# Causal masks of two attention chunks, first tile of each unit: from a GpSimd select to a VectorE minimum, with a new set of order offsets

## The chip, the cores and the metric

The kernel runs on one core of one Trainium2 chip. The metric is the device time of one execution in microseconds. The median of five runs before the change is 925.9 us (924.85 to 927.38).

A core has five engines with an instruction queue each, worked in order: TensorE (PE in the profile; its weight loads are shown as PEld), VectorE (DVE), ScalarE (ACT), GpSimd (POOL) and SyncE (SP, which here only issues transfers). They wait for each other through semaphores.

## What is computed

Two layers, each an attention mixer and an MLP with residuals, on 2048 tokens of width 576, in bfloat16. The attention has 32 heads of width 18, is causal, and each query sees its own key and the 255 before it. Cut to what matters:

```python
def _A_ref(x, wqkv, wo):                    # H = 32, Dh = 18, W = 256
    qkv = (x @ wqkv).reshape(B, S, 3, H, Dh).transpose(2, 0, 3, 1, 4)
    q, k, v = qkv[0], qkv[1], qkv[2]
    scores = einsum("bhqd,bhkd->bhqk", q, k) * Dh ** -0.5
    mask = (idx[:, None] - idx[None, :] >= 0) & (idx[:, None] - idx[None, :] < W)
    p = softmax(where(mask, scores, -1e9))
    return einsum("bhqk,bhkd->bhqd", p, v) ... @ wo
def _B_ref(x, w1, b1, w2, b2):              # F = 4608
    return gelu(layernorm(x) @ w1 + b1) @ w2 + b2
x = x + _A_ref(layernorm(x), ...)
x = x + _B_ref(layernorm(x), ...)           # and both once more
```

## The kernel before

**Tiling.** The tokens are cut into 16 tiles of 128, and the tiles into four chunks of four. With two layers there are eight chunks of work, k = 0 to 7; 0 to 3 are the first layer. Weights of the attention stay in SBUF, those of the MLP are streamed by SyncE.

**Attention of one chunk** (function `E`). The heads are taken in eight groups of four. For each group the query and key tiles that meet are packed into three units of up to 512 columns. Scores are computed transposed, with keys on the partitions and queries along the columns. A unit runs through four engines:

- TensorE computes scores (L757) of four heads into two pairs of PSUM banks. Three pairs exist, and the last can also be taken by other work.
- ScalarE takes the exponential of each pair (L766) into one of three buffers of `pT`, in bf16: 128 keys x 4 heads x up to 512 queries. No maximum is subtracted.
- GpSimd zeroes what the mask excludes (L787): a select by an affine function of partition and column. A 128x128 block needs this where queries and keys are of the same tile ("d", the diagonal) or two tiles apart ("o", the edge of the window). Blocks of one kind that lie side by side go in one select: 128x512 elements for one block (four heads), 128x1024 for two. So a unit has one or two selects; in the code `mi` counts them.
- TensorE multiplies the result with the values (L804, 20 columns: 18 of a head and ones that sum the row). These are the P.V matmuls. At the end of a group VectorE takes the reciprocal (L814) and scales (L819) into `attq`.

The P.V matmuls of a unit are placed two units behind its scores. The scores of the unit three later need its `pT` buffer free again.

**Chunks 0 and 1.** In chunk 0 tiles before the sequence's start are missing, so its three units are 384, 512 and 256 columns wide and have five selects in a group: d and o; d over two blocks, and o; d. Chunk 1 has six: d and o over two blocks; d over two blocks and o; o and d. 368 selects run in all.

**Other work.** `qkv` (L671) makes queries, keys and values; VectorE copies them from PSUM (L710 for queries and keys, L697 for values) and SyncE transposes queries and keys by transfer (L729). `tail` transposes `attq` into `attT` (L848), multiplies with the output weights (L671 again, `wo_sb`), adds the residual on VectorE (L838), takes statistics (L592, L594), 1/sigma on GpSimd (L603, L605), normalises on VectorE (L615, and L620 for a last piece of 64 columns that is wanted twice), and transposes into `xnTm` (L635). The MLP is `G_part` (L881 and L893 on TensorE, the gelu on ScalarE L896) and `mm2` (L922, residual L838, or L841 for the last). Warm-up matmuls (L579) fill gaps that the planner expects on TensorE in the first 140 us.

**What sets the order.** No order is written out by hand. Every piece of work is a task with an engine, a cost and a priority; `Plan.schedule` simulates the engines with these costs and writes down each engine's queue. A priority is a formula plus an offset for the task's stage from the table `PL.nudge`; the stages are named after the chunk (`ea1`, `q2.0`, `t0`, ...). A table of other offsets gives other queues on every engine, with the same tasks. Waits follow from the reads and writes named by each task; an engine's instruction waits until all it names are done, and what stands behind it in its queue waits too.

Of the kernel before, what the change touches and what calls it, by code (L numbers as in the profile page):

```python
# [6 lines left out]
BF16 = mybir.dt.bfloat16  # L7
ACT = mybir.ActivationFunctionType
ALU = mybir.AluOpType
P = 128  # L10
# [398 lines left out]
def build_kernel(nc, A_x, A_wqkv, A_wo, B_x, B_w1, B_b1, B_w2, B_b2, out):  # L409
# [32 lines left out]
    PL = Plan(S, 7)  # L442
    add = PL.add


    PL.nudge = {"b": 1.83, "ea0": -1.98, "ld0+": 40.46, "eb0": 2.23, "q1.0": -6.02, "q1.1": 1.09, "t0": 6.35, "ga0": -26.49, "q2.0": 12.46,
                "q2.2": 12.06, "q2.3": 21.72, "t1": -35.56, "ea2": -3.78, "ga1": -4.7, "ma1": 15.69, "ma1+": -9.39, "q3.2": -1.65, "q3.3": -7.2,
                "eb3": 1.74, "ma2": 3.52, "q4.0": 39.31, "q4.2": 6.69, "q4.3": -1.19, "t3": 50.91, "mb2": 75.66, "mb2+": -12.34, "eb4": 2.23,
                "ma3": 19.38, "q5.3": 4.22, "t4": -3.2, "ln6": 1.17, "ga4": 2.93, "ma4": 3.37, "q6.0": 2.8, "q6.1": 2.68, "q6.3": 11.39, "t5": 14.34,
                "gb4": 5.24, "ln7": 19.99, "ea6": 18.52, "mb4": 22.88, "ma5": 16.32, "q7.0": 16.24, "q7.1": 29.31, "q7.2": 33.42, "q7.3": 24.98,  # L450
                "t6": 73.06, "gb5": 28.24, "mb5": 74.41, "ga6": -3.51, "eb7": -2.5, "t7": -1.07}

    def sb(name, shape, dtype):
        return nc.alloc_sbuf_tensor(name, shape, dtype)
# [21 lines left out]
    vtmp = sb("vtmp", [P, NT], FP32)  # L476
    rstd = sb("rstd", [P, NT], FP32)
    warm = sb("warm", [P, 256], BF16)
    ident = sb("ident", [P, P], BF16)
    b1in = sb("b1in", [NF, P], BF16)  # L480
    nhalf = sb("nhalf", [P, 4], FP32)
# [73 lines left out]
    def x_load(a, cnt, reads, prio):  # L555
# [8 lines left out]
    add("dve", lambda e: e.memset(ident[:, :], 1.0), writes=["ident"], cost=0.15, prio=-11)  # L564
    add("pool", lambda e: e.affine_select(ident[:, :], ident[:, :], pattern=[[-1, P]], compare_op=ALU.is_equal, fill=0.0, base=0,
                                          channel_multiplier=1), writes=["ident"], cost=0.3, prio=-10)
    add("pool", lambda e: e.memset(xn[:, :, D:KD * 128], 0.0), writes=[f"xn{i}" for i in range(NXN)], cost=0.4, prio=-10)
    for i in range(NQN):
        add("pool", lambda e, i=i: e.memset(qn[:, i, :].rearrange("p (h e) -> p h e", e=32)[:, :, DH:32], 0.0),
# [175 lines left out]
    def scores(k, g, parts, prio):  # L745
        l, t0, nt = CH[k]
        T0 = l * NT + t0
        qs, qname = q_of(k)
        sl = pcount[0] % PS
        pcount[0] += 1  # L750
        bs = [Bank(SC, True), Bank(SC, True)]

        def fn(e):
            ins = None
            for (so, qo, nq, col) in parts:
                for j in range(4):
                    ins = e.matmul(two(bs[j // 2])[:, j % 2, col:col + nq * 128], k_of(T0 + so)[0][32 * j:32 * j + 32, g, :],  # L757
                                   qs[32 * j:32 * j + 32, g, qo * 128:(qo + nq) * 128], start=True, stop=True, tile_position=(32 * j, 0))
            return ins
        rd = [f"{qname}{qo + i}" for (so, qo, nq, col) in parts for i in range(nq)] + [k_of(T0 + p[0])[1] for p in parts]  # L760
        ncol = sum(p[2] for p in parts) * 128
        add("pe", fn, reads=rd, writes=bs, cost=0.14 + ncol * 0.00053, prio=prio, lat=0.15, alloc=bs, fifo="pa", after=[f"p{sl}h{h}" for h in range(2)] + [f"p{sl}m{m}" for m in range(3)])
        lo = min(p[3] for p in parts)
        hi = max(p[3] + p[2] * 128 for p in parts)
        for h2 in range(2):
            add("act", lambda e, h2=h2: e.activation(pT[:, sl, 2 * h2:2 * h2 + 2, lo:hi], two(bs[h2])[:, :, lo:hi],  # L766
                                                     ACT.Exp, scale=SCALE),
                reads=[bs[h2]], writes=[f"p{sl}h{h2}"], cost=0.07 + 2 * (hi - lo) * 0.00083, lat=0.17,
                fifo="act", prio=prio)
        blk = {}  # L770
        for (so, qo, nq, col) in parts:
            for q in range(nq):
                if qo + q == so:
                    blk[col + q * 128] = "d"
                elif qo + q == so + 2:
                    blk[col + q * 128] = "o"
        runs = []
        for c in sorted(blk):
            if runs and runs[-1][0] == blk[c] and runs[-1][1] + runs[-1][2] * 128 == c:
                runs[-1][2] += 1  # L780
            else:
                runs.append([blk[c], c, 1])
        for mi, (kind, col, nb) in enumerate(runs):
            sgn = 1 if kind == "d" else -1
            pat = [[0, 4]] + ([[0, nb]] if nb > 1 else []) + [[sgn, 128]]
            ap = pT[:, sl, :, col:col + nb * 128]
            add("pool", lambda e, ap=ap, pat=pat, sgn=sgn, kind=kind: e.affine_select(  # L787
                ap, ap, pattern=pat, compare_op=(ALU.is_ge if kind == "d" else ALU.is_gt), fill=0.0, base=0, channel_multiplier=-sgn),
                reads=[f"p{sl}h0", f"p{sl}h1"], writes=[f"p{sl}m{mi}"], cost=0.12 + 0.475 * nb, prio=prio)
        return sl  # L790
# [307 lines left out]
```

The softmax here doesn't subtract the row's maximum and nothing guards it: scores larger than these inputs give would overflow.

## Time and profile before

| what | us |
|---|---|
| median of five runs | 925.9 |
| the profiled execution, its own time | 927.38 |
| its span, first to last instruction | 925.3 |
| TensorE busy (granted clock 1.00) | 898.5 |
| ScalarE busy | 598.7 |
| GpSimd busy, all | 365.3 |
| GpSimd, 256 selects of 128x512, mean 0.646 | 162.2 |
| GpSimd, 112 selects of 128x1024, mean 1.107 | 123.9 |
| VectorE busy | 317.7 |

How to read it: busy times overlap, since the engines run beside each other, and the two rows of selects overlap slightly at their edges. TensorE is busy for 97% of the span. A line number in the profile is a line of the kernel printed above; `pT<-pT` names the tile written and the one read. An instruction's row shows start and duration in microseconds, its shape, how many equal ones were merged, and in a bracket how long its engine had been idle before it and what ended that.

### The profile page before, as it was taken

How to read it: one execution, taken by the hardware profiler on the slowest of the kernel's cores; microseconds unless marked ns; L12 is line 12 of the kernel's file. 1: busy time of each engine (PE TensorE's matmuls, PEld its weight loads, DVE VectorE, ACT ScalarE, POOL GpSimd, SP SyncE). 2: the span in 40 equal slices, each digit the busy share in tenths (PEclk: the TensorE clock that was granted, in tenths of full speed). 3: DMA queues.
4: the chain of work that ended last, by engine and by line, in shares of the span. 5: the costliest groups of instructions: out<-in, count | busy, mean ns of one | idle time of the engine just before them, and what ended most of it. 6: DMA issues, size and time to landing. Idle time of an engine off the chain costs nothing. (4 is left out here: it accounts for less than half of the span.)

```text
span 925.3 us, 22424 instructions
## 1 busy us (share of the span) xinstructions
PE 898.5 (97%) x9374; PEld 565.9 (61%) x9411; DVE 317.7 (34%) x797; ACT 598.7 (65%) x721; POOL 365.3 (39%) x505
## 2 busy tenths in 40 slices
PE   9899899999999999999999999999999999999998
PEld 6566465665756657577565756656576564657556
DVE  5747121842234403176021723145123520241001
ACT  4877687677836777662777567656686777852541
POOL 3766453553603535061351644315443363610100
PEclk9999999999999999999999999999999999999999
DMA  7797829943295333743639461773519626174430
GB/s 196 145 231 135 191 75 211 223 123 118 49 209 152 117 115 120 168 102 67 208 51 272 66 190 43 171 194 63 199 40 211 155 65 208 37 207 152 150 116 27
DMA packets 204596, 128.85 MB, mean 139 GB/s; under 512 B 128848, under 2 KB 202448, under 8 KB 204496
## 3 DMA queue, kind: packets, MB, share of 16 engines
q1 hardware_dynamic: 199952, 120.06, 51.8%
q0 software_dynamic: 2112, 4.72, 2.0%
q10 hardware_dynamic: 2432, 2.65, 0.9%
q8 instruction: 74, 1.21, 0.5%
q14 instruction: 26, 0.21, 0.1%
HBM read 91.87 MB, written 2.36 MB: 102 GB/s over the span
## 5 line engine op out<-in xcount | busy, mean ns | idle before, releaser
L766 ACT ACTIVATE pT<-ps 128x1024 bf16<-128x1024 f32 (+2 forms) x384 | 348.8, 970 | 120.1 <-PE ps L757 118.8
L787 POOL TENSOR_SCALAR_AFFINE_SELECT pT<-pT 128x512 bf16<-128x512 bf16 (+1 forms) x368 | 281.1, 786 | 269.5 <-ACT pT L766 261.3
L922 PE MATMUL ps<-w_sb,hT 128*128 128x288 bf16 x2304 | 313.7, 286 | 1.8 <-DMA w_sb<-in_B_w_dram 0.9
L896 ACT ACTIVATE hT<-ps,b1col 128x512 bf16<-128x512 f32 x288 | 197.9, 687 | 175.5 <-PE ps L893 173.9
L893 PE MATMUL ps<-xnTm,w_sb 128*128 128x512 bf16 x1115 | 255.0, 379 | 3.0 <-issue 1.7
L922 PEld LDWEIGHTS ps<-w_sb,hT 128*128 128x128 bf16 x2304 | 211.8, 97 | 71.8 <-issue 16.7
L893 PEld LDWEIGHTS ps<-xnTm,w_sb 128*128 128x128 bf16 x1152 | 108.8, 98 | 138.1 <-issue 17.4
L838 DVE TENSOR_TENSOR x_res<-ps,x_res 128x288 f32<-128x288 f32 x160 | 71.2, 449 | 234.5 <-PE ps L922 213.6
L671 PE MATMUL ps<-wqkv,xnTa 128*128 128x288 bf16 x960 | 134.5, 286 | 2.6 <-DVE qn L710 1.6
L804 PEld LDWEIGHTS ps<-vA,pT 128*128 128x128 bf16 x2880 | 94.1, 96 | 26.0 <-POOL pT L787 11.8
L671 PEld LDWEIGHTS ps<-wqkv,xnTa 128*128 128x128 bf16 x960 | 86.9, 97 | 35.8 <-DVE qn L710 6.5
L804 PE MATMUL ps<-vA,pT 128*128 128x20 bf16 x2880 | 100.0, 171 | 4.5 <-POOL pT L787 3.2
L710 DVE CAST qn<-ps 128x288 bf16<-128x288 f32 x120 | 54.1, 454 | 116.2 <-PE ps L671 115.8
L904 POOL TENSOR_TENSOR x_res<-x_res,b2bc 128x576 f32<-128x576 f32 x32 | 40.8, 1275 | 115.6 <-ACT hT L896 115.5
L757 PE MATMUL ps<-qT,kT 32*128 32x384 bf16 (+2 forms) x1216 | 64.0, 276 | 4.1 <-ACT pT L766 3.0
L814 DVE RECIPROCAL rinv<-ps 128x16 f32<-128x16 f32 x64 | 16.2, 253 | 129.2 <-PE ps L804 128.9
L603 POOL TENSOR_SCALAR vtmp<-mv_all 128x1 f32<-128x1 f32 (+1 forms) x43 | 8.8, 204 | 110.8 <-DVE mv_all L594 109.2
L592 DVE BATCH_NORM_STATS2 st_all<-x_res 128x6 f32<-128x288 f32 x104 | 44.8, 448 | 13.7 <-DMA x_res<-in_A_x_dram 12.2
L671 PE MATMUL ps<-wo_sb,attT 128*128 128x288 bf16 x320 | 45.0, 286 | 2.4 <-DVE x_res L838 1.1
L881 PE MATMUL ps<-xnTm,w_sb 64*128 64x512 bf16 x288 | 39.5, 377 | 2.4 <-DMA xnTm<-xn 1.4
L615 DVE TENSOR_SCALAR xn<-x_res,mv_all,rstd 128x576 bf16<-128x576 f32 x52 | 36.8, 713 | 13.2 <-DMA xnTm<-xn 7.5
L757 PEld LDWEIGHTS ps<-qT,kT 32*128 32x128 bf16 x1216 | 19.5, 92 | 34.6 <-issue 18.6
(43 smaller groups left out, 284.3 us busy)
## 6 DMA issues: line engine op xcount, KB each, us to landing
w_sb<-in_B_w_dram SPq DMA_DIRECT2D x48, 864.0 KB, 6.6
w_sb<-in_B_w_dram SPq DMA_DIRECT2D x48, 768.0 KB, 4.8
w_sb<-in_B_w_dram SPq DMA_DIRECT2D x96, 48.0 KB, 4.5
x_res<-in_A_x_dram POOLq DMA_DIRECT2D x4, 1152.0 KB, 8.2
out_dram<-xn SPq DMA_DIRECT2D x16, 144.0 KB, 1.8
wqkv<-in_A_wqkv_dram ACTq DMA_DIRECT2D x3, 576.0 KB, 8.3
hT<-in_A_x_dram SPq DMA_DIRECT2D x2, 576.0 KB, 4.9
wo_sb<-in_A_wo_dram ACTq DMA_DIRECT2D x1, 576.0 KB, 6.6
```

Source lines behind the costliest of these rows:

```text
L592: add("dve", lambda e, i=i, s=s: e.bn_stats(st_all[:, t, i, :], s[:, t, i * HB:(i + 1) * HB]), reads=res, writes=[f"st{t}_{i}"], cost=0.37 ...
L671: ins = e.matmul(bank(bs[o])[:, 0:HB], lhs(c), rhs(c, o * HB), start=(c == 0), stop=(c == KD - 1))
L710: add("dve", lambda e, b=bs[o], dst=dst: e.tensor_copy(dst, bank(b)[:, 0:HB].rearrange("p (h d) -> p h d", d=DH)), reads=[bs[o]], writes=[ ...
L757: ins = e.matmul(two(bs[j // 2])[:, j % 2, col:col + nq * 128], k_of(T0 + so)[0][32 * j:32 * j + 32, g, :], qs[32 * j:32 * j + 32, g, qo * ...
L766: add("act", lambda e, h2=h2: e.activation(pT[:, sl, 2 * h2:2 * h2 + 2, lo:hi], two(bs[h2])[:, :, lo:hi], ACT.Exp, scale=SCALE), reads=[bs ...
L787: add("pool", lambda e, ap=ap, pat=pat, sgn=sgn, kind=kind: e.affine_select(ap, ap, pattern=pat, compare_op=(ALU.is_ge if kind == "d" else ...
L804: ins = e.matmul(bank(B_O)[:, o:o + VW], pT[:, sl, j, col + qi * 128:col + (qi + 1) * 128], vA[:, (T0 + so) % VS, 4 * g + j, :], start=(fi ...
L838: add("dve", lambda e: e.tensor_tensor(x_res[:, t, sl], bank(b)[:, 0:HB], x_res[:, t, sl], ALU.add), reads=[b], writes=[f"x{t}h{hh}"], cos ...
L893: ins = e.matmul(bank(bk)[:, 0:n], w1_sb[:, sl, col:col + 128], xnTm[:, k % 2, c, 0:n], start=False, stop=(c == 3))
L896: add("act", lambda e, ff=ff, fl=fl, bk=bk: e.activation(hT[:, fl, 0:n], bank(bk)[:, 0:n], ACT.Gelu_apprx_tanh, bias=b1col[:, ff:ff + 1]), ...
L904: add("pool", lambda e, t=t: e.tensor_tensor(x_res[:, t, :], x_res[:, t, :], b2bc[:, :], ALU.add), reads=["b2", f"h{fl}"], writes=X(t), co ...
L922: ins = e.matmul(bank(b)[:, 0:HB], hT[:, fl, i * 128:(i + 1) * 128], w2_sb[:, fl, hh * HB:(hh + 1) * HB], start=(fl == 0), stop=(fl == NFH ...
```

## The change

For chunks 0 and 1 (`k <= 1`) the first select of every unit (`mi == 0`) becomes an elementwise minimum on VectorE of the exponentials with a constant tile. The tile `keep` holds 0 where the mask excludes and 3.38e38 elsewhere, one 128x128 plane for "d" and one for "o". Exponentials are not negative, so the minimum with 0 is 0, and the minimum with the large number leaves them as they are. The plane is broadcast over the four heads and over one or two blocks. Both operands are bf16 in SBUF. 48 selects are replaced: 32 of 128x512 and 16 of 128x1024. A second select of a unit stays on GpSimd, as do all of chunks 2 to 7.

`keep` is made at the start by one fill on VectorE and two 128x128 selects on GpSimd. The table of offsets is replaced as a whole, so that the order of tasks differs on every engine, up to where it becomes the same again. The number of matmuls of each shape, of exponentials and of transfers stays.

```diff
-    PL.nudge = {"b": 1.83, "ea0": -1.98, "ld0+": 40.46, "eb0": 2.23, "q1.0": -6.02, "q1.1": 1.09, "t0": 6.35, "ga0": -26.49, "q2.0": 12.46,
...
+    PL.nudge = {"q1.1": -4.02, "q1.2": 0.61, "q1.3": 0.62, "ln2": 8.43, "t0": 2.88, "ga0": -13.55, "q2.2": -0.87, "q2.3": 2.8, "t1": -1.11,
...
+    keep = sb("keep", [P, 2, 128], BF16)
...
+    add("dve", lambda e: e.memset(keep[:, :, :], 3.38e38), writes=["keep"], cost=0.15, prio=-9)
+    for i, (sgn, op) in enumerate(((1, ALU.is_ge), (-1, ALU.is_gt))):
+        add("pool", lambda e, i=i, sgn=sgn, op=op: e.affine_select(keep[:, i, :], keep[:, i, :], pattern=[[sgn, 128]], compare_op=op, fill=0.0,
+                                                                  base=0, channel_multiplier=-sgn), writes=["keep"], cost=0.3, prio=-7)
...
         for mi, (kind, col, nb) in enumerate(runs):
+            if (k <= 1) and (mi == 0):
+                ap = pT[:, sl, :, col:col + nb * 128].rearrange("p j (n c) -> p j n c", n=nb)
+                m = keep[:, 0 if kind == "d" else 1, :].unsqueeze(1).unsqueeze(1).to_broadcast([P, 4, nb, 128])
+                add("dve", lambda e, ap=ap, m=m: e.tensor_tensor(ap, ap, m, ALU.min), reads=[f"p{sl}h0", f"p{sl}h1", "keep"],
+                    writes=[f"p{sl}m{mi}"], cost=0.02 + 0.28 * nb, lat=0.14, prio=prio)
+                continue
```

## The prediction

> **What bounds the kernel now.** I read the page's first part, then the chain, then TensorE's idle time by stretch, then the rows of VectorE and GpSimd where they run together.
>
> ```profile
> PE 898.5 (97%) x9374; PEld 565.9 (61%) x9411; DVE 317.7 (34%) x797; ACT 598.7 (65%) x721; POOL 365.3 (39%) x505
> PE 29%; DVE 1%; DMA 1%; POOL 1%; issue 0%; ACT 0%; POOLq 0%
> L787 POOL TENSOR_SCALAR_AFFINE_SELECT pT<-pT 128x512 bf16<-128x512 bf16 (+1 forms) x368 | 281.1, 786 | 269.5 <-ACT pT L766 261.3
> ```
>
> TensorE is busy 898.5 of 925.3 us: only 26.8 us can be won without changing its work, and the change leaves that work alone (as many matmuls of each shape). GpSimd's 281.1 us of masks lie off the path unless a P.V matmul (L804) waits for one. So the question is where the 26.8 us lie.
>
> ```profile
> core 0: us, PE busy (x) PEld busy (x) DVE busy (x) ACT busy (x) POOL busy (x), PEclk, DMA share, GB/s
> 20.00:67.30 47.30, 43.37 (x634) 28.99 (x631) 28.09 (x78) 39.32 (x54) 32.39 (x46) 1.00 0.88 178
> 67.30:98.36 31.06, 26.33 (x390) 18.43 (x388) 22.67 (x56) 23.09 (x24) 22.14 (x32) 1.00 0.83 140
> 98.36:620.00 521.64, 513.10 (x5335) 318.98 (x5358) 178.19 (x447) 346.54 (x416) 204.95 (x275) 1.00 0.56 141
> 620.00:925.30 305.30, 297.50 (x2878) 186.07 (x2892) 77.38 (x186) 181.40 (x216) 98.48 (x129) 1.00 0.44 125
> ```
>
> I cut at 67.30, where chunk 0's last P.V matmul ends, and at 98.36, where the first MLP matmul starts. TensorE idles 47.30 - 43.37 = 3.93 us in the first stretch and 31.06 - 26.33 = 4.73 us in the second, almost a third of all its idle time in 78 us. There no MLP work can fill gaps, and exactly there the masks change. The second stretch in TensorE's order of time:
>
> ```profile
> 78.12 0.55 PE L804 MATMUL ps<-vA,pT 128*128 128x20 bf16 x16 [0.65 <-DVE attq L819]
> 86.82 0.56 PE L804 MATMUL ps<-vA,pT 128*128 128x20 bf16 x16 [1.15 <-POOL pT L787]
> 94.17 0.40 PE L757 MATMUL ps<-x_res,kT 32*128 32x256 bf16 x8 [1.13 <-ACT pT L766]
> 98.36 0.82 PE L881 MATMUL ps<-xnTm,w_sb 64*128 64x512 bf16 x6 [1.44 <-DMA xnTm<-xn]
> ```
>
> The bracket is TensorE's idle time before the row and what ended it: 1.15 us is a mask, 1.44 us the transpose that ends chunk 0's tail.
>
> **The start.** The new constant tile costs VectorE a fill (0.17 us, as `ident`'s) and GpSimd two 128x128 selects (0.29 us each, as `ident`'s L565). They stand around the first rstd, which is over at 5.47, while its reader on VectorE starts at 7.11 behind statistics of a later load: 1.6 us of cover against 0.6; without that cover all 0.6 would show. But two more warm-up matmuls stand ahead of the first transposes (37, not 35). The 35 took 6.53 us, 0.187 each; they end at 7.64 and the transposes began at 7.58. So +0.37 us, taken as **+0.4**.
>
> **What goes from GpSimd.** Of each unit of chunks 0 and 1 the first select goes: 32 of 128x512 and 16 of 128x1024, by the forms' means of 0.65 and 1.11 us some 38 us. For one head group of chunk 0 the three units' masks took 1.23 (two 512s), 1.69 (1024 and 512) and 0.63: 3.55 us.
>
> **What VectorE gets.** 48 TENSOR_TENSOR with both inputs bf16 in SBUF: no row of the trace is one. Fast bound: the bf16 normalisation (L615 from hT, 576 elements) takes 0.41 and a 64-element L620 0.22 when nothing holds them; 0.37 ns an element gives 0.39 us for 512 and 0.58 for 1024. Slow bound: from L814 (16 elements, 0.25) to L710 (288, 0.45) 0.74 ns an element: 0.62 and 1.00. I take the fast ones, whose row has the same types and place. Beside one GpSimd select of 0.63 that starts on the same exponential, a group's masks then end after 0.63 + 0.63 + 0.39 = 1.65 us, by the slow bound 0.63 + 1.00 + 0.62 = 2.25, if the two engines run side by side.
>
> Whether they do is the open price:
>
> ```profile
> 84.86 1.90 POOL L787 TENSOR_SCALAR_AFFINE_SELECT pT<-pT 128x512 bf16<-128x512 bf16 x2
> 84.55 0.22 DVE L620 TENSOR_SCALAR xn<-x_res,mv_all,rstd 128x64 bf16<-128x64 f32 x1
> 85.73 1.08 DVE L620 TENSOR_SCALAR xn<-x_res,mv_all,rstd 128x64 bf16<-128x64 f32 x1
> ```
>
> The same 64-element instruction takes 0.22 us before the selects start and 1.08 beside them; it ends at 86.81, the selects at 86.76, and these take 1.90 us where a pair takes 1.69. So a one-input VectorE instruction is held until a select ends. A two-input one may be held not at all (0) or behind its whole sibling (0.63). Held each time, a group's masks take 1.02 + 1.21 + 0.39 = 2.62 us (slow bound 3.50), still under 3.55: held or not, the mask is not later than before; what a hold costs is VectorE's time, and what is queued behind. The casts that free TensorE's banks stand there (L710, L697), and the residuals and normalisations of the tail. I take half of the mins held.
>
> This is where a rule speaks against the change. The Trainium skill, page "SBUF — State Buffer", section "Who interferes with whom", says that a VectorE instruction with two SBUF inputs contends with a GpSimd instruction that reads SBUF, and that the later one blocks fully until the first ends. By it every min that meets a select is held or holds it, so the sum would be nearer the slower rival below than my half; the rows above show such holding for a one-input instruction only, and none for this kind.
>
> **Chunk 0 (20 to 67).** With 1.65 to 2.6 us of mask in a group in place of 3.55, the three score buffers come round sooner. The floor is not far: ScalarE needs 39.32 of the 47.30 us. (Work between two points of TensorE's order is counted here and below at the rates of its dense runs: 0.123 us for a 288-column matmul, from 132 in 16.17 us; 0.39 us for 16 P.V matmuls; 0.33 us for a full unit's eight scores.) The new order puts 25 fewer QKV matmuls between the second group's end and chunk 0's last P.V (85, not 110; 25 x 0.123 = 3.1 us of work that only moves behind it). TensorE's own work there falls to 43.37 - 3.1 = 40.3, so it and ScalarE nearly balance, and little more than half of the 3.93 us can go. I take **-2.0** (bounds -3.9 and 0).
>
> **Chunk 0's tail and chunk 1's first half (67 to 98).** The select in front of the 1.15 us wait has one sibling fewer ahead of it: gone. For the 1.44 us: the last out-projection matmul came at 85.7, the first MLP matmul 12.7 us later, with 8.5 us of TensorE work between. In the new order 16.6 us of work stand between (25 QKV moved there, the out-projection placed earlier). On the SyncE queue attT's four transposes go out in one run, with one normalised-input transpose before and two behind them, and the next chunk's query transposes wait behind; nothing there reads an MLP input later than before. But VectorE was busy without a gap from 80 to 94.7, and 12 mins now stand in this stretch (8 of 512, 4 of 1024): 5.4 us fast, 9.0 slow. 22.67 + 5.4 = 28.1 of 31.06 us fits; some 7 of them lie between the tail's first residuals and its last normalisation, 3.3 us, and 12.7 + 3.3 = 16.0 just fits the 16.6. So at best -1.15 - 1.44 = -2.6; holds on half the mins (6 x 0.3 to 0.6) give a part back. I take **-1.5** (bounds -2.6 and +3.6, the second from the rival below).
>
> **After 98.36.** No mask changes there. The order does until TensorE's last 136 of 940 groups, which are equal. The 521.64 us up to 620 hold 8.5 us of idle time: at most half could go, such as 0.96 us at 259 (attT; 4.2 us of work stood between chunk 2's last P.V and its out-projection, now 22.1), while new waits of that size can come. I take **0** (bounds -4 and +4). The second select of each unit and all of chunks 2 to 7 stay as they are.
>
> **Sum.** +0.4 - 2.0 - 1.5 + 0 = -3.1: the span goes from 925.3 to 922.2. The profiled execution took 927.38, 2.1 above its span and 1.5 above the median of the runs, 925.9; I put the change on the median: **922.8**.
>
> **Rivals.**
> *VectorE becomes the bound of the tail (slower).* In 67 to 98 it has 31.06 - 22.67 = 8.39 us free, 0.70 for each of 12 mins. If a min with its hold takes more than 0.70 us, the tail's normalisations, their transposes and the first MLP matmul are late. At 0.45 mean + 0.55 held = 1.0 each that is 12.0 - 8.4 = +3.6 us, and chunk 0's gain is eaten by casts behind held mins: 925.9 + 0.4 + 3.6 = 929.9. For it: the 1.08 us row, and the gapless VectorE. Against it: a short min started first holds the select, which is cheap, and halving GpSimd's masks frees the L620s from waits like that 0.86.
> *The bound is ScalarE and nothing comes of it (same).* In chunk 0 exponentials follow scores closely and four of TensorE's waits there (0.2 to 0.4 us) end with an exponential, not a mask; what a faster mask gives is waited for at the next exponential. Only 0.4 - 0.5 - 0.5 = -0.6: 925.3. Against it: ScalarE's 8 us idle in that stretch.
> *The new order loses later (slower).* Four waits like the 0.96 us one in the 98 to 620 stretch: -3.1 + 4 + 2 of gain not realised = 928.8. Nothing in the counted distances shows one.
> *All goes (faster).* Both stretches lose all they can, and later waits 2: 0.4 - 3.9 - 2.6 - 2 = 917.8.
>
> **How the numbers follow.** This kernel's five runs spread over 0.27%, so 0.2% (1.9 us) is about what can be told from no change. Forecast (921 to 924) 0.43, everything goes 0.08, nothing comes of it 0.21, VectorE bound 0.17, order loses 0.11. So faster 0.51, same 0.21, slower 0.28. The range 918.0 to 929.5 leaves the ends of the first and fourth out.
>
> **What would show it.** Right: the first MLP matmul at 94.5 to 96.5; no mask wait over 0.5 us before it; mins near 0.4 and 0.6 us; GpSimd's busy time down by some 37 us. Wrong: mins over 1 us on average beside selects, a transpose of xnTm still waited for at the first MLP matmul, more than 4.7 us idle between chunk 0's end and it, or new waits of near 1 us between 100 and 620.

## The result, and the profile after

The change made the kernel slower, by 0.3%. Its median is 930.28 us (928.69 to 933.61, 41 runs), that of the kernel before over the runs beside it 927.42 us (924.85 to 932.04, 78 runs); the ratio is 1.0031, 95% interval 1.0023 to 1.0038. Measured once more, beside other executions of the kernel before, it was 1.0050 (1.0031 to 1.0069). The forecast was 922.8 us with a range of 918.0 to 929.5: wrong in sign, and the median lies outside the range.

The profiled execution has a span of 930.2 us (own time 932.06) against 925.3 before: 4.9 us more in the pair of traces, 2.9 us between the medians. Lines of the kernel after are shifted: the minimum is L792, the select L798, exponentials L771, scores L762, P.V L815, QKV and out-projection L676, casts L715 and L702, the residual L849, the first MLP matmul L892.

First the lines of the page that answer to the first fence of the prediction:

```profile
PE 901.9 (97%) x9374; PEld 566.9 (61%) x9411; DVE 340.4 (37%) x846; ACT 598.7 (64%) x721; POOL 337.0 (36%) x459
PE 29%; POOL 1%; DMA 1%; DVE 1%; issue 0%; ACT 0%; DVEq 0%; POOLq 0%
L798 POOL TENSOR_SCALAR_AFFINE_SELECT pT<-pT 128x512 bf16<-128x512 bf16 (+1 forms) x320 | 251.5, 805 | 300.9 <-ACT pT L771 277.6
```

TensorE has 28.3 us of idle time in place of 26.8, and 3.4 us more busy time for the same matmuls. VectorE got 22.7 us more. The selects, by form, took 286.1 us before and 255.3 after: 30.8 us went, not the 38 forecast, mostly because the 128x512 selects that stay take 0.672 us on average in place of 0.646.

Next the stretches, cut as before at chunk 0's last P.V matmul (67.30, now 69.13) and at the first MLP matmul (98.36, now 103.36):

```profile
core 0: us, PE busy (x) PEld busy (x) DVE busy (x) ACT busy (x) POOL busy (x), PEclk, DMA share, GB/s
20.00:69.13 49.13, 42.47 (x603) 27.29 (x601) 36.78 (x95) 39.69 (x54) 17.25 (x22) 0.93 0.78 166
69.13:103.36 34.23, 31.42 (x435) 21.27 (x434) 30.82 (x74) 22.11 (x24) 13.63 (x20) 1.00 0.74 134
103.36:620.00 516.64, 508.19 (x5274) 315.53 (x5298) 179.19 (x446) 345.03 (x416) 198.81 (x261) 1.00 0.57 139
620.00:930.20 310.20, 301.88 (x2920) 189.31 (x2932) 81.54 (x200) 183.39 (x217) 99.43 (x132) 1.00 0.47 130
```

From the first MLP matmul to the end both kernels take the same: 925.3 - 98.36 = 826.9 before, 930.2 - 103.36 = 826.8 after. So the whole loss in time is there by that matmul.

What lies ahead of these marks is not quite the same work, so it has to be counted, here with the prediction's rates (0.123 us for a QKV matmul, 0.39 for 16 P.V). Ahead of chunk 0's end the trace has 227 QKV matmuls, not 252: 3.1 us of work less, and still that end comes 1.83 us later, a loss of 4.9. The next stretch has 30 QKV and 16 P.V matmuls more than before, 4.1 us, and is 3.17 us longer: 0.9 us won. So five QKV and 16 P.V matmuls, 1.0 us, stand ahead of the first MLP matmul that came behind it before, and what follows has 1.0 us less to do and takes as long: 0.9 us lost. The clock column shows 0.93 in chunk 0's stretch, where it was 1.00.

The 4.9 us can be split. TensorE's idle time in the stretch went from 3.93 to 49.13 - 42.47 = 6.66 us (+2.7). The stretch has 27 QKV and two warm-up matmuls less, 3.7 us, so 43.37 - 3.7 = 39.7 us of busy time was due, and it is 42.47 (+2.8). Two of each ran before 20 us instead, which gives 0.6 us back. TensorE in order of time, where both show:

```profile
31.59 0.19 PE L976 MATMUL ps<-ident,b1in 36*128 36x36 bf16 x1 [1.73 <-DMA b1in<-in_B_b_dram]
32.94 1.36 PE L676 MATMUL ps<-wqkv,xnTa 128*128 128x288 bf16 x5
...
42.86 1.38 PE L676 MATMUL ps<-wqkv,xnTa 128*128 128x288 bf16 x5
...
44.86 1.30 PE L676 MATMUL ps<-wqkv,xnTa 128*128 128x288 bf16 x5
...
52.63 0.55 PE L815 MATMUL ps<-vA,pT 128*128 128x20 bf16 x16 [0.48 <-POOL pT L798]
...
84.53 0.56 PE L815 MATMUL ps<-vA,pT 128*128 128x20 bf16 x16 [0.61 <-DVE pT L792]
90.21 0.56 PE L815 MATMUL ps<-vA,pT 128*128 128x20 bf16 x16 [0.69 <-DVE pT L792]
```

The first row is a tiny matmul, the transpose of the MLP's first bias `b1`. The new order puts it ahead of chunk 0's second group; its 9 KB load is issued on SyncE at 26.36, behind the load of four tiles of x. TensorE waits 1.73 us for it. Before, it ran at 38.38 and waited for nothing. The next three rows are five QKV matmuls in 1.30 to 1.38 us, where five take 0.79 in the rows around them. The clock by slices of two microseconds:

```profile
30.00:32.00 2.00, 0.41 (x13) 0.39 (x13) 0.87 (x4) 0.00 (x0) 0.04 (x1) 1.00 1.03 104
32.00:34.00 2.00, 2.00 (x32) 1.23 (x29) 1.49 (x6) 1.18 (x2) 0.00 (x0) 0.57 1.14 125
34.00:36.00 2.00, 2.00 (x25) 1.07 (x23) 1.66 (x4) 1.64 (x3) 0.63 (x1) 0.57 0.00 0
...
42.00:44.00 2.00, 1.88 (x21) 0.98 (x21) 1.46 (x4) 1.47 (x3) 1.65 (x3) 0.63 1.42 404
44.00:46.00 2.00, 2.00 (x22) 1.09 (x21) 2.00 (x6) 1.92 (x3) 0.63 (x1) 0.51 1.39 207
```

The column behind the five engines is the granted clock: 0.57, 0.57, then 0.63 and 0.51, where the kernel before shows 1.00 in every slice from 20 to 110. The trace's own record of the clock has it at 0.50 twice, for 3.41 us from 32.3 and for 3.41 us from 42.5. At half the clock a busy TensorE loses at most half of that, 1.7 us each time (an estimate). The first episode follows the wait for `b1`. All QKV matmuls of the run took 137.0 us busy, against 134.5 before: 2.5 us, most of the busy excess above.

Last the masks of a middle unit of chunk 0, the minimum on VectorE and the select on GpSimd of the same exponentials, then a later pair:

```profile
51.30 0.69 DVE L792 TENSOR_TENSOR pT<-pT,keep 128x1024 bf16<-128x1024 bf16 x1 [0.52 <-ACT pT L771]
51.34 1.15 POOL L798 TENSOR_SCALAR_AFFINE_SELECT pT<-pT 128x512 bf16<-128x512 bf16 x1 [0.76 <-ACT pT L771]
...
97.69 1.25 DVE L792 TENSOR_TENSOR pT<-pT,keep 128x512 bf16<-128x512 bf16 x1
...
97.56 1.10 POOL L798 TENSOR_SCALAR_AFFINE_SELECT pT<-pT 128x1024 bf16<-128x1024 bf16 x1 [2.26 <-ACT pT L771]
```

In the first pair the select starts 0.04 us behind the minimum and ends 0.50 us after it: 0.63 of its own and 0.52 held. In the second the select came first, and a minimum that takes 0.36 to 0.42 alone takes 1.25, to 0.28 us after the select's end. In these pairs whoever is second does most of its work after the first. So the middle unit's masks are over 1.19 us after the exponential (1.69 before), and TensorE waits there again and again for the select, as at 52.63.

### The profile page after: what moved, and what is told of

It reads as the page before. It is cut to its first block, busy times and chain, and to the rows that moved or that the text cites. A ratio compares the mean times of both kernels' runs of the same rounds, so it can differ in the third digit from the quotient of the medians.

```text
span 930.2 us, 22487 instructions
## 1 busy us (share of the span) xinstructions
PE 901.9 (97%) x9374; PEld 566.9 (61%) x9411; DVE 340.4 (37%) x846; ACT 598.7 (64%) x721; POOL 337.0 (36%) x459
## 5 line engine op out<-in xcount | busy, mean ns | idle before, releaser
L771 ACT ACTIVATE pT<-ps 128x1024 bf16<-128x1024 f32 (+2 forms) x384 | 348.8, 970 | 150.0 <-PE ps L762 148.9
L798 POOL TENSOR_SCALAR_AFFINE_SELECT pT<-pT 128x512 bf16<-128x512 bf16 (+1 forms) x320 | 251.5, 805 | 300.9 <-ACT pT L771 277.6
L933 PEld LDWEIGHTS ps<-w_sb,hT 128*128 128x128 bf16 x2304 | 211.2, 97 | 72.9 <-issue 18.7
L849 DVE TENSOR_TENSOR x_res<-ps,x_res 128x288 f32<-128x288 f32 x160 | 71.2, 449 | 216.6 <-PE ps L933 185.4
L676 PE MATMUL ps<-wqkv,xnTa 128*128 128x288 bf16 x960 | 137.0, 289 | 5.2 <-DVE xn L852 1.5
L815 PEld LDWEIGHTS ps<-vA,pT 128*128 128x128 bf16 x2880 | 94.0, 96 | 30.4 <-POOL pT L798 6.6
L676 PEld LDWEIGHTS ps<-wqkv,xnTa 128*128 128x128 bf16 x960 | 87.6, 98 | 38.7 <-issue 6.0
L815 PE MATMUL ps<-vA,pT 128*128 128x20 bf16 x2880 | 100.3, 172 | 6.8 <-POOL pT L798 3.0
L715 DVE CAST qn<-ps 128x288 bf16<-128x288 f32 x120 | 54.0, 453 | 108.2 <-PE ps L676 105.9
L762 PE MATMUL ps<-qT,kT 32*128 32x384 bf16 (+2 forms) x1216 | 64.6, 278 | 3.4 <-ACT pT L771 1.9
L676 PE MATMUL ps<-wo_sb,attT 128*128 128x288 bf16 x320 | 44.7, 286 | 0.7 <-DVE x_res L849 0.7
L892 PE MATMUL ps<-xnTm,w_sb 64*128 64x512 bf16 x288 | 39.5, 377 | 1.2 <-ACT pT L771 0.4
L620 DVE TENSOR_SCALAR xn<-x_res,mv_all,rstd 128x576 bf16<-128x576 f32 x52 | 34.9, 677 | 14.4 <-DMA xnTm<-xn 9.3
L702 DVE CAST vA<-ps 128x288 bf16<-128x288 f32 x64 | 28.9, 455 | 30.7 <-PE ps L676 30.5
```

The source lines that it names most:

```text
L676: ins = e.matmul(bank(bs[o])[:, 0:HB], lhs(c), rhs(c, o * HB), start=(c == 0), stop=(c == KD - 1))
L715: add("dve", lambda e, b=bs[o], dst=dst: e.tensor_copy(dst, bank(b)[:, 0:HB].rearrange("p (h d) -> p h d", d=DH)), reads=[bs[o]], writes=[ ...
L815: ins = e.matmul(bank(B_O)[:, o:o + VW], pT[:, sl, j, col + qi * 128:col + (qi + 1) * 128], vA[:, (T0 + so) % VS, 4 * g + j, :], start=(fi ...
L849: add("dve", lambda e: e.tensor_tensor(x_res[:, t, sl], bank(b)[:, 0:HB], x_res[:, t, sl], ALU.add), reads=[b], writes=[f"x{t}h{hh}"], cos ...
L892: ins = e.matmul(bank(bk)[:, 0:n], w1_sb[64 * b:64 * b + 64, sl, col:col + 128], xnTm[64 * b:64 * b + 64, k % 2, 4, 0:n], start=True, stop ...
L933: ins = e.matmul(bank(b)[:, 0:HB], hT[:, fl, i * 128:(i + 1) * 128], w2_sb[:, fl, hh * HB:(hh + 1) * HB], start=(fl == 0), stop=(fl == NFH ...
```

## The experiments

Ratios are to the kernel before on the same chip, with 95% intervals. Each expectation names its own theories, and the text after it says in words which of them held. "G0" is the start of the first MLP matmul in the profiled run, 98.4 in the kernel before and 103.4 in the one after; between the two orders it compares only to the 1.0 us of work counted above. "Half clock" is the time ahead of G0 for which the trace's record has the clock at 0.50: none in the kernel before, 6.8 us in the one after. A comparison of two traces holds this difference too. Below, "the order of after" or "of before" means that all queues are as in that kernel and only what is named differs.

### The wait for b1

The load is issued on SyncE before the first transposes of normalised input, all else as in the order of after:

```diff
+        i = next(i for i, (st, t) in enumerate(order) if t.writes == ("b1i",))
+        x = order.pop(i)
...
+        sp = [i for i, (st, t) in enumerate(order) if t.eng == "sp" and t.writes == ("q3",)]
+        order.insert(sp[0] + 1, x)
```

> The changed kernel with one load moved: the small load of b1 is issued on SyncE just ahead of the first normalised-input transpose (it was behind a 4-tile load), so that it lands before TensorE reaches the b1 transpose. All other queues as in the changed kernel. Theory 1 (the new order put the b1 transpose ahead of its load, and that wait and the lower clock after it are the loss): no wait before the b1 transpose, no granted clock under 0.95 between 25 and 50 us, 1.7 to 4 us less than the changed kernel's 930.3, so 0.998 to 1.001 of the kernel before. Theory 2 (the minima on VectorE and their holds are the loss): unchanged, 1.002 to 1.004.

928.96 us, ratio 1.0025 (1.0007 to 1.0042); G0 at 101.56, span 927.1. The 1.73 us wait is gone, and one episode of low clock is left (35.3 to 38.7 us) where there were two. G0 comes 1.8 us sooner. By the ratios (1.0031 and 1.0050 with the wait) it is worth 0.5 to 2.3 us, but their intervals overlap. What goes is not the wait's time as such: up to chunk 0's end, 67.33 here, TensorE idles 6.39 us in place of 6.66, since others took its place (0.72 us for `attq` at 32.71 the longest), while its busy time falls from 42.47 to 40.94, about what one low-clock episode costs. G0 is still 3.2 us later than before (2.2 by work), so most stays. The ratio is theory 2's; theory 1's wait was real, but neither its gain nor its clock of 1.00 came.

### Is a minimum worse than a select in its place?

The same queues, but the 48 minima issued as the GpSimd selects that they replaced; once with the late and once with the early load:

```diff
-                add("dve", lambda e, ap=ap, m=m: e.tensor_tensor(ap, ap, m, ALU.min), reads=[f"p{sl}h0", f"p{sl}h1", "keep"],
+                t = add("dve", lambda e, ap=ap, m=m: e.tensor_tensor(ap, ap, m, ALU.min), reads=[f"p{sl}h0", f"p{sl}h1", "keep"],
...
+                t.emit = ("pool", lambda e, ap=ap0, pat=pat0, sgn=sgn, kind=kind: e.affine_select(
+                    ap, ap, pattern=pat, compare_op=(ALU.is_ge if kind == "d" else ALU.is_gt), fill=0.0, base=0, channel_multiplier=-sgn))
```

> The changed kernel's queues on TensorE, ScalarE and SyncE, but the 48 minima are issued as selects on GpSimd at the places that the plan gave the minima. Theory 1: the masks get later again, so slower than the changed kernel by 1 to 4 us: 1.004 to 1.008 of the kernel before. Theory 2: VectorE is relieved and the loss goes: 0.999 to 1.001.

> Both: minima issued as GpSimd selects, and the b1 load issued earlier. Theory 1: between the two other runs, 1 to 4 us above the run with the b1 load alone. Theory 2: as the run with selects alone, at most 0.5 us from it.

937.28 us, 1.0114 (1.0091 to 1.0136), G0 at 108.45; and 938.66 us, 1.0124 (1.0102 to 1.0146), G0 at 106.73. On this order the minima beat the selects that they replaced by 6 to 9 us in all. That refutes theory 2, that the minima are the loss in themselves: the order of after leans on short masks. Theory 1 had the direction, but both runs lie above its ranges. Both have 10.2 us at half clock, against 6.8 and 3.4 with minima, so part of the difference goes through the clock.

### The minima on the order of before

The first selects of chunks 0 and 1 issued as minima, in the queues of before. In the first kernel `keep` was made so early that the first QKV matmul came 0.8 us late; the second makes it later.

```diff
+            if k <= 1 and mi == 0:
...
+                t.emit = ("dve", lambda e, ap=ap4, m=m: e.tensor_tensor(ap, ap, m, ALU.min))
```

> The kernel before with its own queues on TensorE, ScalarE and SyncE, but the first selects of chunks 0 and 1 issued as minima on VectorE at the places that the plan gave the selects. Theory 1: the two mask waits of TensorE before the first MLP matmul (0.2 and 1.15 us) shrink and nothing else grows by as much: 0 to 2 us faster, 0.998 to 1.000. Theory 2: 2 to 4 us slower, 1.002 to 1.004, with waits of TensorE for VectorE casts between 20 and 98 us.

> As the earlier run with the minima in the kernel before's queues, but the constant tile is made later, behind the first normalisations, so that the start isn't late by 0.8 us. Theory A: the start's 0.8 us come back and the rest of the 3 us lost there was casts held behind minima that wait for exponentials: 1.002 to 1.003 of the kernel before, the first QKV matmul at 8.9 us. Theory B: the same number. If the start alone was the loss: 0.999 to 1.001.

930.05 us, 1.0033 (1.0017 to 1.0048), G0 at 102.43; without the late start 929.47 us, 1.0006 (0.9989 to 1.0023), G0 at 100.31. With nothing else changed, the minima bring no gain on the old order, in which selects were the masks. The first result is theory 2's; the second is the last case that the expectation names, the start alone. But the rows of the second kernel, with no half clock, show what eats the gain. The 1.15 us wait for a mask is gone, and two waits for VectorE's other work, queued behind minima, stand there:

```profile
34.01 0.67 DVE L799 TENSOR_TENSOR pT<-pT,keep 128x1024 bf16<-128x1024 bf16 x1
...
35.05 0.43 DVE L716 CAST qn<-ps 128x288 bf16<-128x288 f32 x1
35.54 0.79 PE L677 MATMUL ps<-wqkv,xnTa 128*128 128x288 bf16 x5 [1.16 <-DVE qn L716]
...
86.26 1.31 DVE L799 TENSOR_TENSOR pT<-pT,keep 128x512 bf16<-128x512 bf16 x1
...
88.30 0.56 PE L815 MATMUL ps<-vA,pT 128*128 128x20 bf16 x16 [1.01 <-DVE attq L830]
```

In the kernel before that cast ran at 34.25, and the QKV group waited 0.35 us for it.

### The middle unit's loop

In three groups the middle unit's scores stand straight behind its P.V matmuls, as in the order of before, not behind five QKV matmuls and the next unit's P.V; in a fourth, the first, they only pass five QKV matmuls. The rest is as in the kernel with the early load.

```diff
+            if t.eng == "pe" and t.stage in ('eb0',) and t.fifo == "pa" and t.reads[:1] == ("q1",):
...
+                if seen and j < i - 1:
+                    x = order.pop(i)
+                    order.insert(j + 1, x)
```

> The run with the b1 load issued earlier, and in four head groups of chunk 0's second half the scores of the middle unit stand straight behind the P.V of the same unit of the group before, ahead of 5 QKV matmuls and 8 P.V matmuls; all other queues as there. In the changed kernel these groups repeat every 5.05 us (kernel before: 4.69), because the middle unit's loop (exponentials, mask, P.V, 0.9 us of other TensorE work, scores) closes in 5.05. Theory A (TensorE's order in this loop is what is lost beside the b1 wait): the groups repeat in 4.5 to 4.75 us, chunk 0's last P.V comes 1 to 1.5 us earlier than in that run, and the time falls by 0.8 to 1.5 us. Theory B (VectorE's load and holds are what is lost): the groups gain less than 0.2 us each and the time stays within 0.5 us.

929.62 us, 1.0014 (0.9998 to 1.0029), G0 at 100.88, the clock 1.00 throughout. Chunk 0 ends 1.25 us sooner (66.08, not 67.33), but 1.1 of that is there before the first moved scores (a P.V group at 43.50, not 44.62), where this run has no low-clock episode and the other has one. The first moved group wins 0.6 us and the other three lose 0.5 together. In place of the old wait stand a wait of 0.42 us ahead of the moved scores, ended by an exponential, and in two groups one of 0.37 ahead of a QKV matmul, ended by a cast of VectorE. The chunk's end and the ratio are theory A's, but the groups that are to bring them repeat every 5.15 to 5.3 us, against 5.05, and A had 4.5 to 4.75: the place of the scores is worth next to nothing here.

### VectorE's time, doubled

Every minimum is done twice (the second changes nothing), with the early load:

```diff
+                if t.eng == "dve" and "keep" in t.reads:
+                    self.S.add(t.eng, t.fn, names(t.reads), names(t.writes))
```

> The run with the b1 load issued earlier, with every minimum of the mask done twice in a row (the second changes nothing): VectorE's added load is doubled, about 22 us more. Theory A: VectorE has room, apart from the mask's own length; 48 masks get 0.36 to 0.6 us longer, of which the loop of each group passes on at most one, 0.6 us x 16 groups: 2 to 8 us slower than that run, first from the loop. Theory B: VectorE is already the bound between 70 and 100 us, so 22 us more shows nearly in full: 12 to 20 us slower.

944.62 us, 1.0173 (1.0135 to 1.0210), G0 at 113.79, span 942.2: 15.1 us more than with single minima, for some 29 us of VectorE work (59.6 us of minima in this run, 31.0 in the kernel after). So about half of the added time comes through to the end, which is theory B's range. Not all of it is waiting for VectorE: this run has 17.1 us at half clock (13.65 in one piece from 39.0), against 3.4, and of the 12.2 us at G0, 5.8 are TensorE's longer busy time and 6.4 idle time.

### Without holds

The second selects of chunks 0 and 1 are issued as minima too, so that no select stands beside a minimum. On the order of after with the early load (in two runs, each beside its own executions of the kernel before), with the late load, and on the order of before; there also with every mask of all eight chunks on VectorE. The kernel after was run again beside the last three:

```diff
+            if k <= 1:
...
+                t.emit = ("dve", lambda e, ap=ap4, m=m: e.tensor_tensor(ap, ap, m, ALU.min))
```

> The run with the b1 load issued earlier, with the second selects of chunks 0 and 1 issued as minima on VectorE too, at the places that the plan gave them: GpSimd has no mask beside VectorE there, so nothing is held. Theory A: the masks of a unit follow each other on one engine (0.69 + 0.36 in place of 1.15), so the loop is as long as before and the time stays within 1.5 us. Theory B, with holds as the cost: 1 to 3 us faster; with VectorE's load as the cost: 3 us slower or more.

> The kernel without holds once more, in more rounds and on another chip's baseline: both theories 0.9985 to 1.0010.

> The changed kernel unaltered, beside the next three on one chip. Both theories: 1.002 to 1.004 of the kernel before, first MLP matmul near 103.4 us, idle of 1.73 us ahead of the b1 transpose.

> The changed kernel's queues with the second selects of chunks 0 and 1 issued as VectorE minima too; the b1 load stays where it is, so the 1.73 us wait stays. Theory H (the hold between a minimum and the select beside it is what is left of the loss once the wait for b1 is taken out): 1.2 to 2 us less than the changed kernel, minima of 0.41 (512) and 0.69 (1024) on average, 1.0010 to 1.0022 of the kernel before. Rival S (what is left is the new order of TensorE's loop, masks are short enough): within 0.6 us of the changed kernel.

> The queues of the kernel before, all masks of chunks 0 and 1 issued as VectorE minima, none on GpSimd. Theory H: no hold is left, a group's masks take about 0.41+0.69+0.41 in place of 3.55 us, and scores stand right behind each P.V there: chunk 0's last P.V at 64 to 66.5 us (67.3 before), first MLP matmul at 95 to 97.5 (98.4), 0.998 to 0.9995 of the kernel before, and 1.5 to 3 us less than the queues of before with only the first masks on VectorE. Rival S (ScalarE and the order are the bound in chunk 0, VectorE's queue in its tail): 0.9995 to 1.0015.

> As the last, with every mask of all eight chunks a VectorE minimum; GpSimd keeps no mask. In chunks 2 to 7 the MLP's matmuls fill TensorE, so theory H expects nothing more there: within 0.0012 of the last. Rival V (minima at the places of GpSimd's selects stand in VectorE's queue ahead of casts and wait for exponentials there, and the casts are late): 2 to 6 us slower than the last, with new waits of TensorE ended by VectorE's casts between 100 and 620.

| kernel | median us | ratio (95%) | G0 | half clock, us |
|---|---|---|---|---|
| after's order, early load, no holds | 927.71 | 1.0001 (0.9977 to 1.0024) | 100.77 | 3.4 |
| the same again | 929.09 | 1.0006 (0.9988 to 1.0025) | 100.31 | 3.4 |
| after itself | 932.18 | 1.0050 (1.0031 to 1.0069) | 103.21 | 6.8 |
| after's order, late load, no holds | 930.53 | 1.0025 (1.0009 to 1.0041) | 100.99 | 3.4 |
| before's order, no holds | 928.44 | 1.0015 (1.0001 to 1.0029) | 100.92 | 6.8 |
| before's order, all masks as minima | 931.56 | 1.0039 (1.0022 to 1.0056) | 100.45 | 0 |

VectorE's groups by form, in the kernel after and in the first without holds (L799 there are the first masks, L811 those that were selects); the number behind the busy time is the mean in ns:

```profile
L792 DVE TENSOR_TENSOR pT<-pT,keep 128x512 bf16<-128x512 bf16 x32 | 18.7, 586 | 2.9 <-ACT pT L771 2.9
...
L792 DVE TENSOR_TENSOR pT<-pT,keep 128x1024 bf16<-128x1024 bf16 x16 | 12.3, 769 | 5.4 <-ACT pT L771 5.4
```

```profile
L799 DVE TENSOR_TENSOR pT<-pT,keep 128x512 bf16<-128x512 bf16 x32 | 13.3, 414 | 2.5 <-ACT pT L778 2.5
L811 DVE TENSOR_TENSOR pT<-pT,keep 128x512 bf16<-128x512 bf16 x32 | 13.1, 408 | 0.0
...
L799 DVE TENSOR_TENSOR pT<-pT,keep 128x1024 bf16<-128x1024 bf16 x16 | 11.0, 688 | 4.2 <-ACT pT L778 4.2
```

A 512 minimum falls from 586 to 414 ns without selects beside it, a 1024 one from 769 to 688. On the order of after the holds are worth about 2 us by the ratios, as the theory of holds had it: 1.0025 goes to 1.0001 and 1.0006 with the early load. The intervals overlap; G0, with equal half clock, comes 0.8 and 1.25 us sooner. With the late load 1.0050 goes to 1.0025; that run does not isolate the hold, since in its profile the wait for `b1` was absent, against what was expected (the x load ahead of it landed in 4.2 us, not 5.6). On the order of before the expectation of a gain failed, and its rival S came true: 1.0015, no better than with holds. With all eight chunks' masks on VectorE it is 3.1 us more by the medians, as rival V had it; TensorE's waits for casts and masks grew a little (QKV ended by a query cast 3.0 us in place of 1.7), which fits that rival and does not prove it. After itself came out above what was expected of it, with a wait of 1.97 us for `b1`.

### The limit: no first mask

The first masks of chunks 0 and 1 are left out, on each of the two orders:

```diff
+                if t.emit == 0:
+                    continue
...
+            if k <= 1 and mi == 0:
+                t.emit = 0
```

> The queues of the kernel before, the first masks of chunks 0 and 1 left out altogether (no select, no minimum; the output lacks them). It is the limit of what a mask of no cost could give on that order. Theory V (VectorE's time for minima is what eats the gain): chunk 0's last P.V at 63 to 66 us, first MLP matmul at 94 to 97, 0.996 to 0.999 of the kernel before. Rival O (masks bound little there; exponentials and the order do): chunk 0's last P.V after 66.5, first MLP matmul after 97.5, 0.999 to 1.001.

> The changed kernel's queues with the early b1 load, the first masks of chunks 0 and 1 left out altogether. Theory V: 3 us or more below the same kernel with minima (first MLP matmul at 98.5 or earlier in place of 101.6), 0.998 of the kernel before or less. Rival O (the new order is what is left of the loss): first MLP matmul after 100, within 1.5 us of the kernel with minima, 1.000 to 1.002.

On the order of before: 927.80 us, 1.0016 (1.0007 to 1.0024), chunk 0's last P.V at 68.56 and G0 at 99.56. So on this order a mask that costs nothing gains nothing, as rival O had it. The rows show what came in the masks' place:

```profile
40.41 1.20 SPq L635 DMA_TRANSPOSE xnTa<-xn  x1
40.91 0.97 POOL L536 DMA_DIRECT2D x_res<-in_A_x_dram  x1
```

```profile
38.49 0.97 POOL L540 DMA_DIRECT2D x_res<-in_A_x_dram  x1
39.87 1.20 SPq L639 DMA_TRANSPOSE xnTa<-xn  x1
...
45.70 1.00 PE L675 MATMUL ps<-wqkv,xnTa 128*128 128x288 bf16 x5 [1.56 <-DMA xnTa<-xn]
99.56 0.80 PE L887 MATMUL ps<-xnTm,w_sb 64*128 64x512 bf16 x5 [1.84 <-DMA xnTm<-xn]
```

The first fence is the kernel before, the second the one without first masks. TensorE's waits for selects ahead of P.V fell from 3.2 to 1.3 us over the whole run, but it now waits 1.56 us for the transposed normalised input of a QKV group, which it did not before, and 1.84 for that of the first MLP matmul (1.44 before). The first of these waits seems to go back to GpSimd's queue. With fewer selects ahead of it, GpSimd issues its 1152 KB load of x before that transpose and not behind it, and the transpose, issued 0.54 us earlier, lands 5.8 us after its issue in place of 2.6. Two kernels with minima on this order, the second of the first masks alone and the one without holds, show the same swap (loads at 40.20 and 39.60, transposes at 41.70 and 41.51, landed after 4.9 us), though TensorE does not come to wait for it there. That the load is what holds the transpose up is inferred from this and not tested. Behind the wait the clock is at 0.50 for 3.41 us, from 46.1. TensorE was 0.7 us ahead of the kernel before just ahead of that wait, and is 2.0 behind it at 50.3, where the clock is back.

On the order of after: 924.69 us, 0.9979 (0.9967 to 0.9992), G0 at 95.34, theory V's result. The two stretches, first with minima and early load, then without the first masks:

```profile
20.00:67.33 47.33, 40.94 (x601) 26.99 (x599) 35.67 (x93) 39.50 (x54) 17.33 (x22) 0.96 0.87 171
67.33:101.56 34.23, 31.41 (x435) 21.25 (x434) 30.83 (x74) 22.11 (x24) 13.64 (x20) 1.00 0.74 133
```

```profile
20.00:62.87 42.87, 39.23 (x601) 26.11 (x599) 24.76 (x69) 38.72 (x54) 14.45 (x22) 1.00 0.88 189
62.87:95.34 32.47, 30.47 (x435) 21.54 (x433) 25.07 (x62) 22.36 (x24) 12.39 (x20) 1.00 0.79 143
```

Same queues, same matmuls: the minima cost 4.46 us in the first stretch and 1.76 in the second, 6.2 us by G0. Of the 4.46, 1.7 are TensorE's longer busy time (40.94, not 39.23) in the one low-clock episode, which the run without them lacks; 2.75 are idle time. 2.4 us are given back later (825.5 us from G0 to the end with minima, 828.0 without), where the run without them has its own 3.41 us at half clock, from 182.5. In the first stretch VectorE has 24.76 us of work in place of 35.67.

### Half of the change, planned anew

The minima with the old table of offsets (its diff to the kernel after is below), and the old selects with the new table; the planner makes the queues of both:

```diff
-    PL.nudge = {"q1.1": -4.02, "q1.2": 0.61, "q1.3": 0.62, "ln2": 8.43, "t0": 2.88, "ga0": -13.55, "q2.2": -0.87, "q2.3": 2.8, "t1": -1.11,
...
+    PL.nudge = {"b": 1.83, "ea0": -1.98, "ld0+": 40.46, "eb0": 2.23, "q1.0": -6.02, "q1.1": 1.09, "t0": 6.35, "ga0": -26.49, "q2.0": 12.46,
...
```

> The minima of the changed kernel with the offsets of the kernel before, planned anew. Theory V (the minima cost, wherever they stand): 1.001 to 1.004 of the kernel before. Rival O (the new offsets cost): 0.997 to 1.000. Neither says where the planner puts the rest, so a difference of more than 0.5 per cent either way would be the order's alone.

> The GpSimd selects of the kernel before with the offsets of the changed kernel, planned anew. Theory V: no minimum to pay, and the queues differ from the changed kernel's by the planner's costs of the masks; 0.998 to 1.002 of the kernel before. Rival O: 1.004 to 1.010, since the offsets lean on short masks, as the changed kernel's queues with selects did (1.0114).

936.80 us, 1.0106 (1.0089 to 1.0123); and 939.15 us, 1.0137 (1.0118 to 1.0155). Both lie above what either theory had expected. The first loses before G0 (106.26), the second behind it (G0 at 99.05, and 840.3 us from there to the end, 826.9 in the kernel before). Both have much time at half clock: the first 13.65 us from 39.1, the second 10.2 us behind G0. So neither half of the change can be judged by the other left out: a table of offsets goes with the tasks and costs of its own plan, and the runs on a fixed order are the ones that tell the masks' share.

### The two small gains together

The kernel without holds, with the middle unit's scores moved as above:

> The changed kernel's queues with the early b1 load, all masks of chunks 0 and 1 as minima (no hold), and in four groups the middle unit's scores straight behind its P.V. Theory V (what is left is the masks' delay on that order, without which it gave 0.998): the two small gains add, 0.998 to 0.9995. Rival R (the swap only moves the wait to the casts behind the minima): 0.9995 to 1.0015, as without it.

931.60 us, 1.0041 (1.0019 to 1.0064), G0 at 101.73. They do not add: the result lies above both theories, and above the same kernel without the move, measured beside it (1.0006). Its profile, of a long execution (934.11 us), loses 1.4 us against that one by G0 and 3.7 behind G0, where the queues are the same; 3.41 us at half clock there make at most 1.7 of that, and the rest is open. No version that computes all masks came out faster than the kernel before; the nearest, without holds and with the early load, is level with it.

## Why the prediction was wrong, point by point

**The bound: the premise failed.** The prediction took 3.93 and 4.73 us of idle time before the first MLP matmul as what shorter masks can win. The waits named there were real, but the limit shows that they are not won by shortening the masks: on the old order no first mask at all is 1.0016. Where GpSimd has less to do, it issues a large load earlier, and a transpose that TensorE needs lands 2.7 us later; where VectorE has the masks, its casts and scalings are late. That is the rival "nothing comes of it", whose result was right for that order and whose cause (ScalarE) was not the one the rows show.

**The start, +0.4.** The first QKV matmul came at 8.72, before at 8.90: -0.2. The making of `keep` was covered as said, and the two more warm-up matmuls cost nothing: 37 took 6.09 us, where 35 had taken 6.53.

**The price of a minimum, 0.39 and 0.58 us.** Without a select beside it 0.41 and 0.69: the small one right, the large one 0.11 too cheap. "Half of the mins held" was the weaker choice: wherever the middle unit's pair was looked at, one held the other. Over all 48, 18.7 + 12.3 = 31.0 us, where the fast prices make 32 x 0.39 + 16 x 0.58 = 21.8. The Trainium skill's rule (page "SBUF — State Buffer", section "Who interferes with whom": the later of the two blocks until the first ends), which the prediction had set against its own choice, nearly agrees with the pair at 51.30: a select of 0.63 us ends 0.50 us after the minimum, so all but 0.13 of it came behind.

**Chunk 0, -2.0 (bounds -3.9 and 0): the step that failed.** It came to +4.9, outside bounds that excluded a loss. Three things were left out of the sum. The new order moves the transpose of `b1` ahead of its own load (+1.73 of idle time, though taking that wait out left the idle time nearly as long); the prediction counted the queues' steps elsewhere and did not follow this one. The clock fell twice to one half (about +2.8 of busy time). And "held or not, the mask is not later than before" compared the masks with their old selves, where the new order needed them earlier: against no first mask on that order, the minima cost 4.46 us in this stretch, 2.75 of it idle time.

**Chunk 0's tail and half of chunk 1, -1.5.** It came to -0.9 (34.23 - 31.06 - 4.1; the prediction had counted the 25 QKV matmuls, and the trace has 30 and 16 P.V). The wait for the MLP's transposed input went, as forecast, and the 1.15 us wait for a mask came back as 0.61 and 0.69 for minima. The slower rival's threshold was 0.70 us for each of 12 minima: they took 8.89 us here, 0.74 each, and its sum 12 x 0.74 - 8.39 gives +0.5, which did not come. The rival's time, 929.9, is near the median by luck: its place was chunk 0's tail, and the loss lies in chunk 0.

**After 98.36, 0.** It came to -0.1 in time, to +0.9 by work.

**What is shown, and what is open.** On the order of after, with the early load, the ladder is 1.0124 with selects, 1.0025 with minima beside selects, 1.0001 and 1.0006 with minima alone, 0.9979 with no first mask. The first step, and the one from minima beside selects to no mask, are clear of the intervals; those in between overlap. So the first masks' length costs time on this order. It was laid out around masks shorter than the chip's, which can be read off: the planner reckons a minimum at 0.30 or 0.58 us (0.02 + 0.28 for each block), and it took 0.586 and 0.769 on average, while its 0.595 and 1.07 for a select were near the measured 0.646 and 1.107. That this error is why the offsets failed is argued and not shown: no table of offsets planned with corrected costs was measured. Why the clock fell in some profiles and not in others (two episodes before 50 us in after, one with the early load, none with the moved scores) is open too, and with it how the 4.9 us of the profiled pair shrink to 2.9 between the medians. How much of the loss is the clock's is not separated from the waits that come before its falls.

## What to carry to other kernels

Before crediting a faster operation with the waits that it ends, leave it out altogether and see what stands behind: here that limit was zero on the old order, and its trace has GpSimd, with less to do, issuing a large load ahead of a transfer that mattered. Moving half of a tile's masks to a second engine beside the first made the pairs looked at run one after the other, so a planner does better with the held duration than with the lone one. When an order is laid out anew, follow every instruction that passes another, the unimportant ones first: TensorE stood 1.73 us before a 36x36 transpose.

## What the hardware showed that was not expected

The granted clock drops without a long pause. In after, by slices of 2 us, it read 0.57 from 32 to 36 us, behind a slice in which TensorE was busy 0.41 of 2 us, and 0.63 and 0.51 from 42 to 46, behind a slice with 1.44 of 2 us busy and no wait over 0.4. The Trainium skill, page "TensorE: Matmul & The Clock Gate", Part 1, describes a gate that passes all pulses or half of them by a window of some 3.4 us, and tells of micro-idling that makes it swing as well as of long gaps. The traces agree with the window: wherever their record of the clock is under 1.00, the last microseconds of the span apart, it is 0.50, for 3.41 us or for two or four times that (6.83 in the run with selects, 13.65 in the one with doubled minima). But in the kernel with the moved scores slices as thin (1.43, 1.51 and 1.42 of 2 us, one after the other from 38 us) left the clock at 1.00, so the share of busy time alone does not tell when it falls.
